# Batch 1 of a 2-D Fourier transform is loaded through a copy in DRAM, the first products change places, and every unit gets a new kind and new due times

## The chip, the cores and the metric

The kernel runs on one core of a Trainium2 chip. Its time is the device time of one execution in microseconds (us); the median of three runs before the change is 599.53 us (598.72 to 600.61). TensorE multiplies matrices, VectorE, ScalarE (ACT) and GpSimd (POOL) work on tiles in the on-chip memory, and SyncE (SP) issues most transfers.

## What is computed

The input x has 8 batches of 3008 rows with 256 numbers. Each batch goes through a 2-D Fourier transform, of which the real part is kept, and then every row goes through a gated feed-forward network (FFN) with 1536 hidden numbers:

```python
X = np.fft.fft(x, axis=1)
X = np.fft.fft(X, axis=2)
x = X.real.reshape(24064, 256)
g = x @ w_gate
out = (g / (1 + np.exp(-g)) * (x @ w_val)) @ w_out
```

## The kernel before

**Transform.** A real transform along 3008 rows has mirror symmetry, so rows are needed in rising and in falling order. For each batch the tile XA takes 128 row pairs of each of four quarters (R = 752 rows): its slots 0 to 3 hold the rising rows, 4 to 7 the falling ones. The partitions run in falling order of the rows, in blocks of LA = 8, so that the rising rows (up_block) are loaded block by block, 8 partitions a transfer (16 transfers of 64 KB), while the falling rows (down_set) take one transfer of 256 KB for each quarter. XC holds the 60 row pairs that remain, in blocks of 4 partitions (15 transfers of 32 KB), even batches in the partitions from 0 and odd ones in those from 64. Batch 1 is an exception: its rows of XC lie in both halves of the partitions, one of each pair of rows in either, which took a copy XC<-XC within the chip at the end (L169). C1_ORDER and A1_ORDER spell the order in which its 25 and 20 transfers are issued.

POOL folds these rows (fold_steps, L171: cross into SDf, even and odd into EOf, ab into Af, ce and bb into the coefficient tiles CEa, BBa and Fc). Fc goes to the stacks St by transfers. TensorE multiplies the coefficients by tables of sines and cosines (Tab), and VectorE adds and subtracts the results into the tiles Pt and Qt (L1411, the puts), the even and odd parts along the 256 numbers. The second transform, along the 256 numbers, is multiplied into the weights: Wp = CD x W and Wq = SDt x W, and Wm = -2 Wq outside of partition 0 (L1442 to L1457 for the later weights; first_w, L499, for the first).

**FFN.** The 12032 columns of Pt and Qt are cut into 24 tiles (480, 512 or, at the end, 320 wide; 8 more columns join the last). A unit is a tile and one of 12 blocks of 128 hidden numbers; there are 288, in order. Each column gives two output rows, a row k of the transform and its mirror. For one unit TensorE adds Wp x Pt and Wq x Qt into g (gate) and v (value), and then Wm x Qt, which turns the sum into the mirror's. ACT applies silu to g (sp, and sv for the mirror), VectorE multiplies sp by v into hp (L1186), and makes the mirror's value from es (L1109, L1175). POOL multiplies the two halves of sv into hm (L1183) for two units at once. TensorE then multiplies hp and hm by Wo into o (L1236), ACT copies o to ev (L1243) and SP stores it (L1249).

KINDS (L928) has one character for each unit, which says how its work is shared out. A "w" is a unit without these shortcuts (6 products on TensorE). For a hex digit, bit 0 (seeded): ACT writes a first row's term into v ahead of the product (L1045) and copies es, in place of a VectorE operation. Bit 1 (gate split): TensorE leaves out one of the three gate products, and VectorE does two operations instead (L1088, L1152). 4 and above: ACT copies v, and POOL makes hp (L1192); 8: POOL makes the mirror's value as well (L1195).

**Order.** The first stage, up to tile 0, is written out by hand (L517 to L649). All later work is given to a planner (Sched, L767): each operation has an engine, an assumed duration and a due time, which is the planned TensorE time so far plus SHIFT for its sort plus BIAS for its sort and tile. The planner walks through the operations and emits, for each engine, one fixed order; on the chip, each engine follows its order and waits for semaphores. There are 3 buffers of g and v, 2 of o in PSUM, 2 of sv and es, 3 of sp, sg and ev. SP has at most 8 transfers under way in this plan. Transfers for weights (load_w, L386; Wo, L1641) are issued on POOL's queue.

In the first stage psC holds two o buffers until VectorE has read them. half_folded(1, 0, False) is the last table product that needs POOL's EOb, row0 adds the row of the heads CEa and CEc, even_copy copies half of the sums to od, and first_puts makes Pt and Qt of tiles 0 and 1. copies are the copies of the first weights out of PSUM.

Of the kernel before, what the change touches and what calls it, by code (L numbers as in the profile page):

```python
# [19 lines left out]
def kernel(  # L20
# [113 lines left out]
    C1_EARLY = 6  # L134
    C1_ORDER = "uuduuduuduuduumuueuueuece"
    A1_ORDER = "uuuuduuuuduuuuduuuud"

    def load_a(b, q):
        X3 = XA.rearrange("p a q d -> p a (q d)")
        res = ([lambda h=h: q.dma_start(out=X3[LA * h:LA * (h + 1), 0:4, :],  # L140
                                         in_=up_block(b, JA - LA * h, LA)) for h in range(NA)] +
                [lambda a=a: q.dma_start(out=X3[:, 4 + a, :], in_=down_set(b, a, JA, LA, NA)) for a in range(4)])
        return in_order(A1_ORDER, u=res[:NA], d=res[NA:]) if b == 1 else res

    def in_order(order, **todo):
        todo = {k: list(v) for k, v in todo.items()}
        return [todo[k].pop(0) for k in order]

    def load_c(b, q):

        X3 = XC.rearrange("p a q d -> p a (q d)")
        p0 = 64 * (b % 2)
        pm = p0 + NCR
        r = slice(p0, p0 + NCR)
        ups = [lambda h=h: q.dma_start(out=X3[p0 + LC * h:p0 + LC * (h + 1), 0:4, :],
                                       in_=up_block(b, JC - LC * h, LC)) for h in range(NC_)]
        mid = [lambda: q.dma_start(out=XC[pm:pm + 1, 0:4, 1],
                                   in_=rows_at(b, 0, [[R * D, 1], [R * D, 4], [1, D]]))]
        if b != 1:
            return ups + [lambda a=a: q.dma_start(out=X3[r, 4 + a, :], in_=down_set(b, a, JC, LC, NC_))  # L160
                          for a in range(4)] + mid

        def down(a, k):
            q.dma_start(out=XC[0:NCR, 4 + a, 0] if k else XC[r, 4 + a, 0],
                        in_=rows_at(b, R * (a + 1) - 2 * JC + k, [[2 * LC * D, NC_], [-2 * D, LC], [1, D]]))

        downs = [[lambda a=a, k=k: down(a, k) for a in range(4)] for k in range(2)]
        return in_order(C1_ORDER, u=ups, d=downs[0], e=downs[1], m=mid,
                        c=[lambda: q.dma_start(out=XC[0:NCR, 0:4, 1], in_=XC[r, 0:4, 0])])  # L169
# [311 lines left out]
    def half_folded(eo, a0, first):  # L481
        for q in range(2):
            for a in range(a0, a0 + 2):
                dst, rhs = set_cols(acc[eo][q], Tab[:, 0, q, eo], a)
                nc.tensor.matmul(dst, EOb[:, eo, a, q, :], rhs, start=first and a == a0, stop=False, skip_group_check=True)
# [58 lines left out]
    for hi in range(2):  # L544
        q.dma_start(out=X3c[64 * hi + NCR:64 * hi + 64, :].rearrange("p (c d) -> p c d", d=D),
                    in_=zeros[64 * hi + NCR:64 * hi + 64].unsqueeze(1).to_broadcast([64 - NCR, 16, D]))
    loads_c1 = load_c(1, q)
    for load in loads_c1[:C1_EARLY]:
        load()
# [22 lines left out]
    half_folded(1, 0, False)  # L572
    load_w(1, (1,))
    heads(Ec0[:, 0], Ec0[:, 1], CEc)
# [167 lines left out]
    )  # L742
    BIAS = {(t, k): v for t, row in enumerate(BIAS_ROWS) for k, v in zip(SHIFT, row)}
# [11 lines left out]
    W_AT = (0.0, 2.0, 3.2, 4.6)  # L755
# [164 lines left out]
    def pool_us(n):  # L920
# [14 lines left out]
        "001601031052",  # L935
        "300171700001",
        "331213005030",
        "010271031001",
        "34130b310300",
        "01b300700101",  # L940
        "21312101b300",
        "001371310011",
        "32120011b212",
        "10130b135030",
        "000135003170",
        "033170001011",
        "213b21011200",
        "103b10319610",
        "4030b13300b0",
        "616404563200",  # L950
        "143034169230",
        "706150233313",
# [343 lines left out]

    def run_loads(n):
        for what, k, fn in loads[:n]:
            up = k < (NA if what[0] == "A" else NC_)
            r, w, us, ring = [], [((what[0],), k)], 0.4 if up else 0.62, 0.57 if up or what[0] == "C" else 1.14  # L1300
            if what == ("A", 1):
                r = [(("C",), C1_ORDER.rindex("u"))]
                us, ring = (0.42, 0.75) if A1_ORDER[k] == "u" else (0.75, 1.1)
            if what == ("C", 1):
                us, ring = (0.48, 0.75) if C1_ORDER[k] == "u" else (0.95, 1.0)
                if C1_ORDER[k] == "c":
                    r = [(("C",), j) for j, o in enumerate(C1_ORDER) if o == "u"]
            S.add("SP", us, fn, r=r, w=w, after=[(("A",), "pre" if A1_ORDER[k] == "d" else "preW")] if what == ("A", 1) else [],
                  lat=2.5, ring=ring)
        del loads[:n]  # L1310
# [4 lines left out]
    def fold_step(what, i, unit):  # L1315
        kind, b = what
        q, j = (1, i) if what == ("C", 1) else divmod(i, 6)
        if i == 0:
            run_loads(max((k + 1 for k, (w_, _, _) in enumerate(loads) if w_ == what), default=0))
# [14 lines left out]
        r = {0: [((kind,), k) for k in range(40)], 1: [(tmp, "F")], 2: [(tmp, "F")], 3: [(tmp, "E"), (tmp, "O")],  # L1334
# [12 lines left out]
    def load_next(what):  # L1347
        kind, b = what
        if kind == "A":
            if b + 1 < B:  # L1350
                loads.extend((("A", b + 1), k, fn) for k, fn in enumerate(load_a(b + 1, nc.sync)))
        else:
            b = b // 2 * 2 + 2
            if b < B:
                loads.extend((("C", b), k, fn) for k, fn in enumerate(load_c(b, nc.sync) + load_c(b + 1, nc.sync)))
# [248 lines left out]
    for k in range(C1_EARLY):  # L1604
        S.add("DMA", 0.01, lambda: None, w=[(("C",), k)], lat=2.0)
# [3 lines left out]
    S.add("DMA", 0.01, lambda: None, w=[(("pq", 0), "Q")], lat=0.1)  # L1609
# [7 lines left out]
    for i, u in enumerate(units):  # L1617
# [49 lines left out]
    S.run({'DVE': 1.6, 'ACT': 1.0, 'POOL': 1.4, 'PE': 0.0, 'SP': 2.0})  # L1667
# [30 lines left out]
```

## Time and profile before

| | |
|---|---|
| median of 3 runs | 599.53 us |
| the profiled execution | 600.4 us |
| its span, first to last instruction | 598.6 us |
| DMA packets, bytes | 51082, 57.65 MB |
| HBM read, written | 29.43 MB, 24.65 MB |

The profile is of one execution. For each engine it gives the busy time; TensorE's matmuls overlap, so that its starts say more than its ends. A row of the timeline has the start and the length, the engine (PE is TensorE, PEld its weight loads, DVE VectorE, SPq SyncE's queue), the line, the tiles out<-in, the shapes and the count; in brackets stands the idle time of the engine before it and what ended it. A row by stretch has, after the stretch and its length, the busy time of PE, PEld, DVE, ACT and POOL with their counts, then the granted TensorE clock (1.00 is full), the busy share of the DMA engines and GB/s. A row of waits has the total, how many there were and the longest.

### The profile page before, as it was taken

To read this page: it belongs to the slowest core of one execution; us is meant where nothing else is said; L and a number is where in the kernel's file an instruction comes from. 1 tells how busy PE (TensorE), PEld (TensorE's weight loads), DVE (VectorE), ACT (ScalarE), POOL (GpSimd) and SP (SyncE) were. 2 spreads that over 40 slices of the span, in tenths; PEclk is the share of its full clock that TensorE was granted. 3 is DMA by queue.
4 is the path that set the end of the run, shared out by engine and by line. 5 is a ranking of instruction groups with operands and counts; after the bars stand their busy time and mean duration, and the time that the engine had idled before them with its cause. 6 is when DMAs were issued, how large, how long until landed. Compare 5 with 4: busy or idle time off the path is not lost.

```text
span 598.6 us, 12468 instructions
## 1 busy us (share of the span) xinstructions
PE 587.0 (98%) x3953; PEld 389.2 (65%) x4012; DVE 570.3 (95%) x1064; ACT 557.4 (93%) x1080; POOL 527.8 (88%) x486
## 2 busy tenths in 40 slices
PE   7999999999999999999999999999999999999997
PEld 5456666666666666666666666666666666666686
DVE  8989999999999999999999999999999999999993
ACT  8778989989998999999999999999999999999995
POOL 8977999999899999998999998897986868687772
PEclk9999999999999999999999999999999999999999
DMA  9956347454715523454127122046221202111212
GB/s 247 150 110 115 109 121 141 132 140 117 178 46 107 136 70 113 123 129 138 57 55 166 46 62 82 19 115 161 63 64 37 65 19 80 48 46 53 60 54 81
DMA packets 51082, 57.65 MB, mean 96 GB/s; under 512 B 7283, under 2 KB 38439, under 8 KB 51017
## 3 DMA queue, kind: packets, MB, share of 16 engines
q1 hardware_dynamic: 47433, 53.91, 35.2%
q0 software_dynamic: 3216, 2.36, 2.8%
q8 instruction: 31, 0.51, 0.4%
q10 hardware_dynamic: 368, 0.59, 0.3%
q14 instruction: 34, 0.28, 0.2%
HBM read 29.43 MB, written 24.65 MB: 90 GB/s over the span
## 4 chain that ended last, share of the span: by engine, by line
PE 71%; ACT 8%; DMA 6%; DVE 4%; POOL 3%; issue 3%; SPq 1%; ACTq 0%; POOLq 0%; DVEq 0%
PE o L1236 30%; PE g L972 19%; PE v L972 16%; DMA XA<-in_x_dram 5%; ACT sv L1159 2%; PE o L1394 2%; PE g L1394 2%; ACT v L1045 2%; ACT es L1107 1%; POOL hm L1183 1%; DVE sv L1175 1%; ACT sp L1084 1%; DVE hp L1186 1%; ACT sp L1156 1%; ACT ev L1243 1%
## 5 line engine op out<-in xcount | busy, mean ns | idle before, releaser
L1183 POOL TENSOR_TENSOR hm<-sv 128x1024 bf16<-128x1024 f32 (+2 forms) x137 | 254.7, 1862 | 44.1 <-ACT sv L1159 17.7
L1175 DVE SCALAR_TENSOR_TENSOR sv<-es,v 128x512 f32<-128x512 f32 (+2 forms) x262 | 173.6, 668 | 5.4 <-PE v L972 2.8
L1236 PE MATMUL o<-Wo,hm 128*128 128x256 bf16 (+1 forms) x1128 | 163.6, 273 | 0.3
L1236 PE MATMUL o<-Wo,hp 128*128 128x256 bf16 (+1 forms) x1104 | 159.7, 273 | 0.2
L1186 DVE TENSOR_TENSOR hp<-sp,v 128x512 bf16<-128x512 f32 (+2 forms) x233 | 154.2, 668 | 2.8 <-PE v L972 2.0
L1236 PEld LDWEIGHTS <-hm 128*128 128x128 bf16 (+2 forms) x1140 | 111.8, 98 | 57.9 <-issue 2.5
L1236 PEld LDWEIGHTS <-hp 128*128 128x128 bf16 (+2 forms) x1140 | 111.9, 98 | 55.8 <-issue 0.9
L1159 ACT ACTIVATE sv<-g 128x512 f32<-128x512 f32 (+2 forms) x179 | 116.7, 671 | 4.6 <-PE g L972 2.3
L1084 ACT ACTIVATE sp<-g 128x512 f32<-128x512 f32 (+2 forms) x179 | 110.5, 621 | 4.1 <-PE g L972 2.7
L972 PE MATMUL v<-Pt,Wp 128*128 128x512 bf16 (+2 forms) x288 | 105.4, 375 | 1.8 <-DVE hp L1186 0.5
L972 PE MATMUL g<-Pt,Wp 128*128 128x512 bf16 (+2 forms) x280 | 104.4, 374 | 0.9 <-ACT sv L1159 0.7
L1045 ACT ACTIVATE v<-bc,w 128x512 f32<-128x512 bf16 (+2 forms) x146 | 104.6, 717 | 0.4
L1109 DVE SCALAR_TENSOR_TENSOR es<-bc,w,v 128x512 f32<-128x512 bf16 (+2 forms) x128 | 92.6, 731 | 2.4 <-ACT bc L1595 0.8
L1107 ACT ACTIVATE es<-v 128x512 f32<-128x512 f32 (+2 forms) x146 | 90.0, 618 | 3.8 <-PE g L972 1.0
L972 PE MATMUL g<-Qt,Wq 128*128 128x512 bf16 (+2 forms) x247 | 90.5, 374 | 0.4
L972 PEld LDWEIGHTS <-Wp 128*128 128x128 bf16 x576 | 56.3, 98 | 27.8 <-DVE Wp L505 0.7
L972 PE MATMUL g<-Qt,Wm 128*128 128x512 bf16 (+2 forms) x186 | 69.8, 375 | 0.2
L1088 DVE SCALAR_TENSOR_TENSOR sg<-bc,w,g 128x512 f32<-128x512 bf16 (+2 forms) x95 | 68.4, 723 | 1.4 <-PE g L972 0.7
L1159 ACT ACTIVATE sv<-sg 128x512 f32<-128x512 f32 (+2 forms) x95 | 65.1, 692 | 0.2 <-DVE sg L1152 0.2
L1152 DVE SCALAR_TENSOR_TENSOR sg<-sg,g 128x512 f32<-128x512 f32 (+2 forms) x95 | 62.9, 662 | 1.5 <-PE g L972 0.8
L1156 ACT ACTIVATE sp<-g 128x512 f32<-128x512 f32 (+2 forms) x95 | 57.7, 608 | 5.5 <-DVE sg L1152 5.3
L972 PE MATMUL v<-Qt,Wm 128*128 128x512 bf16 (+2 forms) x159 | 59.4, 374 | 0.8 <-ACT es L1107 0.4
(218 smaller groups left out, 759.1 us busy)
## 6 DMA issues: line engine op xcount, KB each, us to landing
out_dram<-ev SPq DMA_DIRECT2D x96, 128.0 KB
XA<-in_x_dram SPq DMA_DIRECT2D x30, 256.0 KB
XA<-in_x_dram SPq DMA_DIRECT2D x112, 64.0 KB
XC<-in_x_dram SPq DMA_DIRECT2D x28, 120.0 KB
XC<-in_x_dram SPq DMA_DIRECT2D x105, 32.0 KB
bc<-br SPq DMA_DIRECT2D x19, 128.0 KB
St<-Fc SPq DMA_DIRECT2D x12, 128.5 KB
out_dram<-ev SPq DMA_DIRECT2D x12, 120.0 KB
```

Source lines behind the costliest of these rows:

```text
L972: nc.tensor.matmul(ps[:, :n], Wt[:, gv, fs], src[:, :n], start=start, stop=stop, skip_group_check=True)
L1045: nc.scalar.activation(T_[kv][:, :w], bc[t][:, :w], AF.Copy, scale=w0[:, 1, f:f + 1])
L1084: nc.scalar.activation(sp_to()[:, :w], T_[kg][:, :w], AF.Silu)
L1088: nc.vector.scalar_tensor_tensor(T_[keg][:, :w], bc[t][:, :w], w0[:, 0, f:f + 1], T_[kg][:, :w], op0=Alu.mult, op1=Alu.add)
L1107: nc.scalar.activation(T_[kes][:, :w], T_[kv][:, :w], AF.Copy, scale=2.0 if on_pool(u) > 1 else 1.0)
L1109: nc.vector.scalar_tensor_tensor(T_[kes][:, :w], bc[t][:, :w], w0[:, 1, f:f + 1], T_[kv][:, :w], op0=Alu.mult, op1=Alu.add)
L1156: nc.scalar.activation(sp_to()[:, :wp], T_[kg][:, :wp], AF.Silu)
L1159: nc.scalar.activation(sv()[:, f % 2, w - 1::-1, 1], T_[kgm if by_dve else kg][:, :w], AF.Silu)
L1175: nc.vector.scalar_tensor_tensor(sv()[:, f % 2, w - 1::-1, 0], T_[kes][:, :w], 2.0, T_[kv][:, :w], op0=Alu.mult, op1=Alu.subtract)
L1183: nc.gpsimd.tensor_tensor(hts_(t)[1][:, f - 1:f + 1, :w], sv()[:, :, :w, 1], sv()[:, :, :w, 0], op=Alu.mult)
L1186: nc.vector.tensor_tensor(hts_(t)[0][:, f, :wp], T_[ksp][:, :wp], T_[kv][:, :wp], op=Alu.mult)
L1236: nc.tensor.matmul(st["ps"][:n, j, :], hts[t][minus][:, f, c:c + n], Wo[:, f, :], start=(f == 0), stop=(f == nF - 1))
```

## The change

- **Loads of batch 1.** The rising rows of XA (four copies of 256 KB, one for each quarter) and of XC (four of 120 KB) are copied within DRAM into a scratch tile in which the blocks lie in falling order (turn). XA's rising half then comes in two transfers of 128 partitions (up_a1), XC's in two of 60 (up_c1), straight into the partitions where they belong, so the copy XC<-XC goes. The falling rows stay as they were. Together SP issues 25 transfers in place of 45. The planner gets new durations for all loads.
- **Their place.** Ahead of tile 0 SP issues one of the two clearing transfers, the middle row, four falling loads of XC and the other clearing transfer, where it was both clearing transfers and six loads. The four other falling loads, the eight copies, the two loads of turned XC and XA's six follow in the plan.
- **First stage.** half_cast(0, 2) goes ahead of the two copies of FA. The first value weight's product goes ahead of half_folded(1, 0), which is split by q with row0 in between; its copy (copies[2], VectorE) goes ahead of the Qt sums; turn_signs goes later. On POOL, heads goes ahead of load_w(1, (1,)).
- **Units.** KINDS and BIAS_ROWS are replaced as a whole (the old BIAS_ROWS stays in the file and is overwritten), as are W_AT and the planner's starting times.

```diff
+    def turn(kind, q):
+        L, N, j0 = (LA, NA, JA) if kind == "A" else (LC, NC_, JC)
+        t = scratch[kind] = dram.tile([4, N, 2 * L, D], F32, name=f"turned{kind}")
+        def one(a):
+            q.dma_start(out=t[a].rearrange("h r d -> r h d"),
+                        in_=rows_at(1, R * a + 2 * j0 - 1, [[D, 2 * L], [-2 * L * D, N], [1, D]]))
+        return [lambda a=a: one(a) for a in range(4)]
...
+    def up_a1(a, q):
+        q.dma_start(out=XA.rearrange("p a q d -> p a (q d)")[:, a:a + 2, :],
+                    in_=scratch["A"][a:a + 2].rearrange("a h (i q) d -> (h i) a (q d)", q=2))
+    def down_c1(a, k, q):
+        q.dma_start(out=XC[slice(0, NCR) if k else slice(64, 64 + NCR), 4 + a, 0],
+                    in_=rows_at(1, R * (a + 1) - 2 * JC + k, [[2 * LC * D, NC_], [-2 * D, LC], [1, D]]))
+    def up_c1(k, q):
+        q.dma_start(out=XC[slice(64, 64 + NCR) if k else slice(0, NCR), 0:4, 1],
+                    in_=scratch["C"][:].rearrange("a h (i q) d -> q (h i) a d", q=2)[k])
...
     half_cast(0, 0)
+    half_cast(0, 2)
     for a in range(2, 4):
         nc.scalar.copy(FA[:, a, :, P + 1:D], psA[a][:, :, P + 1:D])
-    half_cast(0, 2)
...
+    clear_c(1)
+    mid_c(1, q)
+    for a in range(4):
+        down_c1(a, 0, q)
+    clear_c(0)
...
+    copies = [first_w(0, 0, 1, psG.tile([P, T], F32, name="g"))]
     folded_c(0, 0)
-    copies = [first_w(0, k, 1, p_.tile([P, T], F32, name=n_)) for k, (p_, n_) in enumerate(((psG, "g"), (psV, "v")))]
+    copies.append(first_w(0, 1, 1, psV.tile([P, T], F32, name="v")))
...
-    half_folded(1, 0, False)
+    copies.append(first_w(1, 0, 0, psO.tile([P, T], F32, name="o")))
+    heads(Ec0[:, 0], Ec0[:, 1], CEc)
     load_w(1, (1,))
-    heads(Ec0[:, 0], Ec0[:, 1], CEc)
...
-    for i in range(2):
-        row0(0, i, acc[1][i])
     copies[0]()
     copies[1]()
+    copies[2]()
+    half_folded(1, 0, False, (0,))
+    row0(0, 0, acc[1][0])
+    od1 = even_copy(1)
+    half_folded(1, 0, False, (1,))
+    row0(0, 1, acc[1][1])
+    copies.append(first_w(1, 1, 1, psO.tile([P, T], F32, name="o")))
+    first_puts(1, od1, (0,))
+    copies[3]()
     turn_signs()
-    od1 = even_copy(1)
-    copies += [first_w(1, k, k, psO.tile([P, T], F32, name="o")) for k in range(2)]
-    first_puts(1, od1, (0,))
-    for c in copies[2:4]:
-        c()
     first_puts(1, od1, (1,))
...
-    W_AT = (0.0, 2.0, 3.2, 4.6)
+    W_AT = (0.0, 2.4, 3.4, 4.6)
...
-        "06ww20001013",
-        "031303160011",
-        "000010312133",
-        "010210112012",
-        "10110b103133",
+        "02ww60003010",
+        "030001330100",
+        "310130310112",
+        "111010000010",
+        "53130b103113",
...
         if i == 1:
-            loads.extend((("C", 1), k, fn) for k, fn in enumerate(loads_c1) if k >= C1_EARLY)
+            c1 = load_ops("C", 1)
+            loads.extend(c1[:4] + turn_ops("C") + turn_ops("A") + c1[4:])
         if i == A1_LOAD:
-            loads[0:0] = ((("A", 1), k, fn) for k, fn in enumerate(load_a(1, nc.sync)))
+            loads[0:0] = load_ops("A", 1)
...
-    S.run({'DVE': 1.6, 'ACT': 1.0, 'POOL': 1.4, 'PE': 0.0, 'SP': 2.0})
+    S.run({'DVE': 1.4, 'ACT': 0.8, 'POOL': 1.6, 'PE': 0.0, 'SP': 2.0})
```

More of the change, by code (lines that the diff above doesn't have):

```diff
@@ L152, in load_c @@
         p0 = 64 * (b % 2)
[L153 to L169, printed above, removed]
+        return ([lambda h=h: q.dma_start(out=X3[p0 + LC * h:p0 + LC * (h + 1), 0:4, :], in_=up_block(b, JC - LC * h, LC))
+                 for h in range(NC_)] +
+                [lambda a=a: q.dma_start(out=X3[p0:p0 + NCR, 4 + a, :], in_=down_set(b, a, JC, LC, NC_)) for a in range(4)] +
+                [lambda: mid_c(b, q)])
     def fold_steps(eng, X, CE, BB, q, r):
@@ L479, in set_cols, with half_folded @@
         return ps[:, 0:NCE], tab[:, 0:NCE]
-    def half_folded(eo, a0, first):
-        for q in range(2):
+    def half_folded(eo, a0, first, qs=(0, 1)):
+        for q in qs:
             for a in range(a0, a0 + 2):
@@ L1318, in fold_step @@
         if i == 0:
-            run_loads(max((k + 1 for k, (w_, _, _) in enumerate(loads) if w_ == what), default=0))
+            run_loads(max((k + 1 for k, (w_, _, _) in enumerate(loads) if w_ == what or kind == w_[0] == "C"), default=0))
         def fn():
@@ L1333, in fold_step @@
         tmp = ("fold",)
-        r = {0: [((kind,), k) for k in range(40)], 1: [(tmp, "F")], 2: [(tmp, "F")], 3: [(tmp, "E"), (tmp, "O")],
+        r = {0: [((kind,), k) for k in [(i, j) for i in range(2) for j in range(20)] + list(range(20))], 1: [(tmp, "F")], 2: [(tmp, "F")], 3: [(tmp, "E"), (tmp, "O")],
              4: [(tmp, "A")], 5: [(tmp, "E"), (tmp, "O")]}[j]
@@ L1350, in load_next @@
             if b + 1 < B:
-                loads.extend((("A", b + 1), k, fn) for k, fn in enumerate(load_a(b + 1, nc.sync)))
+                loads.extend(load_ops("A", b + 1))
         else:
@@ L1354, in load_next @@
             if b < B:
-                loads.extend((("C", b), k, fn) for k, fn in enumerate(load_c(b, nc.sync) + load_c(b + 1, nc.sync)))
+                loads.extend(load_ops("C", b) + load_ops("C", b + 1))
     def spread_op(b):
@@ L1603 @@
     S.hold("st", 0)
-    for k in range(C1_EARLY):
-        S.add("DMA", 0.01, lambda: None, w=[(("C",), k)], lat=2.0)
+    S.add("DMA", 0.01, lambda: None, w=[(("C",), 19)], lat=4.0)
     for fc in (1, 2):
```

96 lines of the change are left out of this document (51 added, 45 removed), and 24 rows, old and new, of the table BIAS_ROWS.

## The prediction

> **What bounds the kernel now.** I read the page's totals first, then the busy times by stretch, then who TensorE waited for, and last the timeline around each wait.
>
> ```profile
> span 598.6 us, 12468 instructions
> PE 587.0 (98%) x3953; PEld 389.2 (65%) x4012; DVE 570.3 (95%) x1064; ACT 557.4 (93%) x1080; POOL 527.8 (88%) x486
> ```
>
> ```profile
> 0.00:18.86 18.86, 15.77 (x104) 9.90 (x106) 16.42 (x68) 14.73 (x25) 17.29 (x40) 1.00 0.89 220
> 18.86:40.00 21.14, 20.83 (x123) 10.07 (x123) 18.86 (x38) 16.95 (x35) 18.56 (x32) 1.00 0.77 135
> 40.00:60.00 20.00, 19.84 (x129) 12.90 (x131) 19.21 (x33) 16.34 (x31) 14.81 (x16) 1.00 0.67 116
> 60.00:120.00 60.00, 58.11 (x394) 38.56 (x396) 56.92 (x105) 54.13 (x106) 59.37 (x57) 1.00 0.50 126
> 120.00:580.00 460.00, 457.20 (x3081) 304.85 (x3129) 449.50 (x803) 443.92 (x858) 411.95 (x341) 1.00 0.33 85
> ```
>
> In each row the second figure is TensorE's busy time, POOL's the sixth. From 18.86 us, where the FFN starts, TensorE hardly stops: 0.6% idle from 120 to 580, but 1.89 of 60 us from 60 to 120, where POOL is full (59.37 of 60). So the time is the first stage (18.86), all products at full pace, and few waits. A change can pay by fewer products, an earlier start, or by removing those waits. The largest of TensorE's own there:
>
> ```profile
> PE g L972 <- ACT sv L1159: 0.7, 1, 0.7
> PE v L972 <- DVE hp L1186: 0.5, 1, 0.5
> PE v L972 <- ACT es L1107: 0.4, 1, 0.4
> ```
>
> A matmul's modelled end overlaps its follower, so idle time understates a wait; I take start-to-start instead:
>
> ```profile
> 19.29 0.36 PE L972 MATMUL g<-Qt,Wq 128*128 128x480 bf16 x1
> 19.89 0.38 PE L972 MATMUL v<-Pt,Wp 128*128 128x480 bf16 x1 [0.24 <-DVE Wp L505]
> 20.11 0.37 PE L972 MATMUL v<-Qt,Wq 128*128 128x480 bf16 x1
> 20.31 0.37 PE L972 MATMUL g<-Qt,Wq 128*128 128x480 bf16 x1
> ...
> 25.05 0.39 PE L1442 MATMUL o<-XA,CD 128*128 128x512 bf16 x1
> 25.50 0.37 PE L972 MATMUL v<-Pt,Wp 128*128 128x480 bf16 x1
> ...
> 63.66 0.38 PE L1591 MATMUL g<-Qt,sel 128*128 128x512 bf16 x1
> 64.74 0.38 PE L972 MATMUL g<-Pt,Wp 128*128 128x512 bf16 x1 [0.70 <-ACT sv L1159]
> 64.96 0.38 PE L972 MATMUL g<-Qt,Wq 128*128 128x512 bf16 x1
> ...
> 79.72 0.59 PE L972 MATMUL v<-Pt,Wp 128*128 128x512 bf16 x2
> 80.86 0.38 PE L972 MATMUL v<-Pt,Wp 128*128 128x512 bf16 x1 [0.55 <-DVE hp L1186]
> ...
> 106.33 0.57 PE L972 MATMUL g<-Qt,Wq 128*128 128x480 bf16 x2
> 107.25 0.36 PE L972 MATMUL v<-Qt,Wm 128*128 128x480 bf16 x1 [0.36 <-ACT es L1107]
> ```
>
> Undisturbed starts lie 0.20 us apart at 480 columns and 0.22 at 512. So the waits are 0.60-0.20 = 0.40 at 19.89, 0.45-0.22 = 0.23 at 25.50, 1.08-0.22 = 0.86 at 64.74, 1.14-0.44 = 0.70 at 80.86 and 0.92-0.41 = 0.51 at 107.25: 2.70 us in all. The two large ones have one root:
>
> ```profile
> 42.33 2.36 POOL L178 TENSOR_TENSOR SDf<-XC 128x1020 f32<-128x1020 f32 x1 [2.06 <-DMA XA<-in_x_dram]
> 44.92 0.82 POOL L1546 COPY Tab<-Tab 64x752 bf16<-64x752 bf16 x1
> ...
> 53.57 0.20 POOL L202 TENSOR_TENSOR Fc<-EOf 128x2 bf16<-128x2 f32 x1
> 59.65 2.36 POOL L178 TENSOR_TENSOR SDf<-XA 128x1020 f32<-128x1020 f32 x1 [2.03 <-DMA out_dram<-ev]
> 62.11 1.90 POOL L1183 TENSOR_TENSOR hm<-sv 128x1024 bf16<-128x1024 f32 x1
> 64.05 0.64 ACT L1159 ACTIVATE sv<-g 128x512 f32<-128x512 f32 x1 [0.88 <-PE g L1591]
> 78.93 1.29 DVE L1175 SCALAR_TENSOR_TENSOR sv<-es,v 128x512 f32<-128x512 f32 x2 [0.71 <-POOL hm L1183]
> ```
>
> POOL stood 2.06 and 2.03 us in front of batch 1's folds, whose inputs are the loads that the change rebuilds (the semaphore named in the second is another transfer's; only XA is new to that instruction). hm then ends at 64.01, sv comes free, ACT starts at 64.05, and TensorE gets its g buffer. At 78.93 DVE again waits for an hm.
>
> **The change part by part.** *Products.* Counting the unit codes, 95 units were gate-split and 89 are; each split saves one gate product and costs VectorE two operations. Nine 512-wide splits go; two of 512 and one of 320 come. Net 7 x 0.217 - 0.14 = +1.38 us of TensorE, with nothing to hide it. The same count gives VectorE 11 operations fewer (at 0.66 about 7 us of 570), ACT 6 fewer, POOL 4 more (5 us of 528, most in tiles 10 and 21, where POOL has idle time).
>
> *First stage.*
>
> ```profile
> 16.82 0.48 PE L485 MATMUL g<-Tab,EOb 128*128 128x377 bf16 x2
> 17.23 0.33 PE L613 MATMUL v<-Tab,CEa 128*1 128x189 bf16 x2
> 17.73 0.33 PE L613 MATMUL g<-Tab,CEc 128*1 128x189 bf16 x2
> 17.98 0.60 PE L502 MATMUL o<-W,CD 128*128 128x512 bf16 x2
> ```
>
> Two products at 0.16 from 16.82 end at 17.14, two at 0.08 from 17.73 at 17.89: about 0.2 us of gaps, which the new order fills (the value weight's first product goes ahead, and CEc is made before POOL's weight issue). All products are the same, so the FFN starts near 18.66: -0.2 (bounds 0 and -0.3). Wp's value half is now copied before the Qt sums, with VectorE free from about 17.7, so the 0.40 wait goes: -0.4 (bounds 0, -0.4).
>
> *Weights.* POOL issues the last three weight loads behind two small operations more (both heads, like L461 here):
>
> ```profile
> 15.81 0.73 POOL L391 DMA_DIRECT2D XA<-in_moe_w_val_dram  x1
> 16.57 0.21 POOL L461 TENSOR_TENSOR CEc<-Ec 128x2 bf16<-128x2 f32 x1
> ...
> DMA to landing us min/median/max: 7.4/8.2/9.8
> ```
>
> The first of them was out at 15.81 and lands after 7.4; at 16.15 it lands at 23.55. In the new order its product follows 16 products of 0.20 and four of 0.22, at 18.66+4.1 = 22.8. TensorE's order is fixed, so everything behind would stand 0.75 us, or 0 if the load gets faster because SP issues less: I take +0.4. The later 0.23 (the next weights) is then covered: -0.23.
>
> *Loads of batch 1.* SP issued 25 transfers for XC and 20 for XA; now 9 for XC at first hand, 4+4 copies within DRAM (480 KB and 1 MB), 2 loads of turned C, 4 falling and 2 turned A loads: 25. No row shows a copy within DRAM. Its bounds are the pace of the wide early transfers, 220 GB/s (first row above), and that of the 64 KB blocks that go:
>
> ```profile
> 48.24 3.60 SPq L140 DMA_DIRECT2D XA<-in_x_dram  x4
> ...
> Wo<-in_moe_w_out_dram POOLq DMA_DIRECT2D x1, 768.0 KB, 12.0
> ```
>
> 256 KB in 3.60 us is 73 GB/s. 1.5 MB of copies then take 7 or 21 us; behind 11 issues from 13.92 (0.9 each) they start near 23.5. I take about 11 us, since they share the engines with Wo until 35 but are wide; then 2.6 MB at some 200 GB/s: XC by 38, XA near 50 (bounds 43 and 66). Setup keeps POOL until 42.33-2.06 = 40.27, and 41.1 with the table copy (0.82 at 44.92) that now comes ahead of C's fold; the fold with one hm inside took 53.77-42.33-0.82 = 10.6, so POOL asks for XA at 51.7. Both waits, 4.1 us, are then gone. XA's fold comes some 8 us earlier than 59.65. Behind SP's wait for the copies stand the XA loads, C2's loads and the first stores, whose three ev buffers ACT fills; the first store was not needed before 55. So -0.86, -0.70 (bounds 0 and these), and half of 0.51: ACT was late there, and by the codes it loses some 3 us of work in tile 2 and gains as much in tile 3: -0.25 (bounds 0, -0.51).
>
> *Due times of all units.* They can't be costed row by row. Outside these waits TensorE's idle time is 0.6%, 2.8 us from 120 to 580; VectorE's 7 us less lets me take -0.2 (bounds -1.2 and +1.5, half of that idle time either way).
>
> The sum: 1.38-0.2-0.4+0.4-0.23-0.86-0.70-0.25-0.2 = -1.06. The profiled execution took 600.4 (span 598.6), so 599.3; it lay 0.9 above the median of the runs, so **598.4 us**.
>
> **The rivals.** *The loads come late (slower).* If XA lands after 51.7, POOL stands in order, hm behind it, then sv, g and TensorE as at 64.74. Before it lost 4.1 us there and TensorE 1.56; from about 56 on it is worse than before. At the 116 GB/s of the 40-to-60 row the 4.1 MB from 23.5 need 35 us: 58.5, 7 us lost, 3 more than before, plus the 1.38, less 0.4: about 603.4. For it: that row's pace, and Wo's 12 us. Against: those were narrow blocks. In the Trainium skill, "DMA: Bandwidth & Descriptors", section "Anatomy of one DMA", a transfer carries about 2 us of fixed cost, most of it the receipt of the last write, heaviest where the target is HBM; by that estimate the second hop adds about 2 us once (XA at 52), too little for this rival. No row here shows such a receipt by itself.
>
> *The waits stay, from VectorE and ACT.* At 95% and 93% they may hold TensorE wherever POOL did; then only 1.38-0.4 is left: 600.5. Against: the chain of 64.05 starts at hm.
>
> *ACT in tile 5.* Its codes go from 10110b103133 to 53130b103113, about three ACT operations more (2 us), in a stretch where ACT has none to spare:
>
> ```profile
> 140.00:160.00 20.00, 19.84 (x135) 13.13 (x137) 18.67 (x39) 19.94 (x40) 19.67 (x19) 1.00 0.58 127
> ```
>
> If half isn't absorbed, 599.4.
>
> *All goes.* The unit order also closes half of the late idle time and no weight is late: 598.4-1.2-0.4 = 596.8.
>
> **How the numbers follow.** About 0.3% (1.8 us) is what a measurement of this kernel can tell from no change, so faster means below 597.7. Forecast 0.40 (its own range 597.2 to 599.6, 0.16 of it below 597.7), all goes 0.26, waits stay 0.13, tile 5 0.07, late loads 0.14. Faster 0.16+0.26 = 0.42; slower 0.14 and a little of waits-stay, 0.16; same 0.42. The range goes from 596.2 to 601.8, which leaves out most of late loads and the best tail.
>
> **What would show it.** Right: SDf<-XC on POOL near 41 and SDf<-XA by 52 without a DMA wait; no TensorE wait over 0.5 us between 60 and 90; FFN start at 18.7; six products more. Wrong: POOL standing at SDf<-XA beyond 56; TensorE waiting for a weight product near 23 by more than 0.8, or for Wo near 41; ACT full and TensorE waiting for es or sv from 135 to 165.

## The result and the profile after

The changed kernel takes 602.65 us (median of 6 runs, 602.27 to 603.84); the kernel before took 600.07 in the same comparison (6 runs, 598.28 to 601.46). The ratio is 1.0049 with an interval of 1.0026 to 1.0072: slower by 0.5%, where 598.4 was predicted. The profiled execution took 603.73.

First the totals of the changed kernel (span, then busy time, share and number of instructions of each engine), and two of the stretches shown before:

```profile
span 602.0 us, 12426 instructions
PE 591.2 (98%) x3958; PEld 390.7 (65%) x4018; DVE 564.8 (94%) x1053; ACT 554.6 (92%) x1074; POOL 532.5 (88%) x490
...
18.86:40.00 21.14, 20.82 (x125) 10.16 (x124) 18.59 (x41) 17.13 (x35) 18.43 (x34) 1.00 0.93 192
120.00:580.00 460.00, 456.55 (x3052) 302.01 (x3102) 443.31 (x787) 438.69 (x844) 413.09 (x341) 1.00 0.33 85
```

VectorE's work fell by 5.5 us (about 7 were counted), and the loads moved up: 192 GB/s from 18.86 to 40, where it was 135. From 120 on TensorE shows 0.8% of idle time, where it was 0.6%; more on that figure below. POOL's folds of batch 1 and TensorE's first FFN products in the timeline:

```profile
45.44 2.35 POOL L186 TENSOR_TENSOR SDf<-XC 128x1020 f32<-128x1020 f32 x1 [3.85 <-DMA XC<-turnedC]
55.96 2.35 POOL L186 TENSOR_TENSOR SDf<-XA 128x1020 f32<-128x1020 f32 x1 [0.22 <-DMA out_dram<-ev]
...
19.42 0.57 PE L1012 MATMUL g<-Pt,Wp 128*128 128x480 bf16 x2
20.26 0.59 PE L1492 MATMUL o<-XA,CD 128*128 128x512 bf16 x2 [0.27 <-ACT Wq L513]
```

XA's fold no longer waits (0.22 in place of 2.03) and comes 3.7 us earlier. XC's fold is 3.1 us later than before, not earlier. The FFN starts at 19.42, not at 18.66, and 0.84 - 0.41 = 0.43 us behind its first two products TensorE waits for an o buffer, where 0.40 at 19.89 was to go. SP's queue shows why XC is late (in the last row, what it waited for):

```profile
13.80 0.77 SPq L553 DMA_DIRECT2D XC<-Z  x1
19.70 0.63 SPq L156 DMA_DIRECT2D XC<-in_x_dram  x1
...
29.52 2.73 SPq L142 DMA_DIRECT2D turnedC<-in_x_dram  x4
...
SPq L156 <- DMA XC<-Z: 5.0, 1, 5.0
```

The middle row (19.70) is written into partitions that the clearing transfer at 13.80 writes too. SP stood 5.1 us for that, and the copies started 6 us later than the 23.5 that I took.

### The profile page after: what moved, and what is told of

The parts are those of the page before. It is cut to its first block, busy times and chain, and to the rows that moved or that the text cites. A ratio compares the mean times of both kernels' runs of the same rounds, so it can differ in the third digit from the quotient of the medians.

```text
span 602.0 us, 12426 instructions
## 1 busy us (share of the span) xinstructions
PE 591.2 (98%) x3958; PEld 390.7 (65%) x4018; DVE 564.8 (94%) x1053; ACT 554.6 (92%) x1074; POOL 532.5 (88%) x490
## 4 chain that ended last, share of the span: by engine, by line
PE 84%; DVE 4%; ACT 3%; issue 3%; DMA 3%; POOL 1%; SPq 1%; ACTq 0%; POOLq 0%; DVEq 0%
PE o L1276 35%; PE g L1012 22%; PE v L1012 19%; PE g L1444 2%; PE o L1444 2%; DVE sv L1215 2%; DMA XC<-in_x_dram 1%; DVE es L1149 1%; ACT sv L1199 1%; ACT es L1147 1%; DMA out_dram<-ev 1%; DVE hp L1226 1%; POOL hm L1223 1%; PE v L1276 1%; PE o L1492 1%
## 5 line engine op out<-in xcount | busy, mean ns | idle before, releaser
L1199 ACT ACTIVATE sv<-g 128x512 f32<-128x512 f32 (+2 forms) x185 | 123.1, 677 | 5.4 <-PE g L1012 3.2
L1124 ACT ACTIVATE sp<-g 128x512 f32<-128x512 f32 (+2 forms) x185 | 115.2, 630 | 3.0 <-PE g L1012 1.7
L1085 ACT ACTIVATE v<-bc,w 128x512 f32<-128x512 bf16 (+2 forms) x141 | 102.1, 725 | 2.8 <-DVE sv L1215 1.4
L1149 DVE SCALAR_TENSOR_TENSOR es<-bc,w,v 128x512 f32<-128x512 bf16 (+2 forms) x133 | 97.3, 736 | 2.4 <-PE v L1012 1.0
L1012 PE MATMUL g<-Qt,Wm 128*128 128x512 bf16 (+2 forms) x195 | 73.0, 376 | 0.5 <-ACT sp L1124 0.3
L1199 ACT ACTIVATE sv<-sg 128x512 f32<-128x512 f32 (+2 forms) x89 | 62.0, 697 | 3.6 <-DVE sg L1192 2.5
L1128 DVE SCALAR_TENSOR_TENSOR sg<-bc,w,g 128x512 f32<-128x512 bf16 (+2 forms) x89 | 64.1, 722 | 0.7 <-PE g L1012 0.5
L1192 DVE SCALAR_TENSOR_TENSOR sg<-sg,g 128x512 f32<-128x512 f32 (+2 forms) x89 | 58.7, 660 | 2.8 <-PE g L1012 2.1
L1012 PEld LDWEIGHTS <-Wq 128*128 128x128 bf16 x435 | 42.4, 98 | 28.8 <-issue 3.0
L1283 ACT COPY ev<-o 128x512 f32<-128x512 f32 x89 | 55.3, 622 | 3.5 <-PE o L1276 3.3
```

The source lines that it names most:

```text
L1012: nc.tensor.matmul(ps[:, :n], Wt[:, gv, fs], src[:, :n], start=start, stop=stop, skip_group_check=True)
L1085: nc.scalar.activation(T_[kv][:, :w], bc[t][:, :w], AF.Copy, scale=w0[:, 1, f:f + 1])
L1124: nc.scalar.activation(sp_to()[:, :w], T_[kg][:, :w], AF.Silu)
L1128: nc.vector.scalar_tensor_tensor(T_[keg][:, :w], bc[t][:, :w], w0[:, 0, f:f + 1], T_[kg][:, :w], op0=Alu.mult, op1=Alu.add)
L1149: nc.vector.scalar_tensor_tensor(T_[kes][:, :w], bc[t][:, :w], w0[:, 1, f:f + 1], T_[kv][:, :w], op0=Alu.mult, op1=Alu.add)
L1192: nc.vector.scalar_tensor_tensor(T_[kgm][:, :w], T_[keg][:, :w], 2.0, T_[kg][:, :w], op0=Alu.mult, op1=Alu.subtract)
```

## The experiments

The theories that the expectations name: T, the loss lies in the new kinds and due times. R, the new loads of batch 1 cost it (the route through DRAM, or their lateness). F, the new order of the first stage costs it. All times are medians, ratios are to the kernel before, run on the same chip beside them.

| kernel | loads | units | first stage | us | ratio, 95% interval |
|---|---|---|---|---|---|
| before, again | old | old | old | 599.79 | 1.0002 (0.9989 to 1.0014) |
| new loads, old units | new | old | old | 598.53 | 0.9982 (0.9972 to 0.9991) |
| old first stage | new | new | old | 602.69 | 1.0049 (1.0031 to 1.0068) |
| changed kernel | new | new | new | 602.65 | 1.0049 (1.0026 to 1.0072) |
| middle row last | new, mended | new | new | 602.40 | 1.0050 (1.0038 to 1.0062) |

**Units against loads, by exchanging them whole.** Two kernels: the changed one with KINDS and BIAS_ROWS of before, and the kernel before with those of the change.

```diff
 # the changed kernel
-        "02ww60003010",
-        "030001330100",
+        "06ww20001013",
+        "031303160011",
...
-        (0.7, -5.05, -12.55, -2.25, 11.45, -27.35, -34.35, 25.8, 26.55, 21.8, 28.65, 3.65, -10.1, -19.05, 5.25, 0.55, 2.45),
...
```

> The changed kernel with the kinds and due times of before (95 gate splits), its new loads and first stage kept. The plan of all engines is made anew from them. Theory T (the loss lies in the new kinds and due times: 1.38 us of products and some 2 us of new waits behind 120 us): 2 to 3.5 us below the changed kernel, so 599 to 600.7 against 602.65, within 0.2% of before. Rival R (the loads of batch 1 cost it): only the products go, 601.3 or more, and the waits in the first 100 us stay.

> The kernel before with the kinds and due times of the change, its old loads and first stage kept. Theory T: 602 to 604 against 600.1 for the kernel before, with the new products and the waits between 150 and 250 us as in the changed kernel. Rival R: 600 to 601.4, the products alone.

They took 626.83 and 613.13 us, ratios 1.0461 (1.0444 to 1.0478) and 1.0227 (1.0214 to 1.0240). Neither theory had expected that. In the stretch from 120 to 580, where neither loads of batch 1 nor the first stage act any more (first row: old units in the changed kernel; second: new units in the kernel before), TensorE is idle for 11.7 and 5.4 us:

```profile
120.00:580.00 460.00, 448.34 (x2953) 287.14 (x2952) 427.64 (x759) 421.78 (x804) 392.29 (x326) 1.00 0.32 83
120.00:580.00 460.00, 454.56 (x3035) 295.19 (x3033) 434.71 (x769) 429.34 (x822) 406.56 (x336) 1.00 0.32 83
```

A set of due times serves the one plan that it was made with: by its code the planner walks through another order as soon as a load's assumed duration differs (this was not run by itself), and 13 to 27 us against the kernel before hang on the exchange. So exchanging them tells nothing on T or R; from here on the finished order of the engines was kept, and instructions were replaced or moved within it.

**The middle row last.** SP's order alone: `clear_c(1), clear_c(0), 4 x down_c1, mid_c`.

```diff
     clear_c(1)
-    mid_c(1, q)
+    clear_c(0)
     for a in range(4):
         down_c1(a, 0, q)
-    clear_c(0)
+    mid_c(1, q)
```

> The changed kernel with SP's early order changed alone: both clearing transfers, then the four falling loads, and the middle row last, so that its wait for the clearing transfer has the falling loads in front of it. All other engines keep their order. SP's standstill from 14.57 to 19.70 should shrink to 1 us or so, the copies start 4 us earlier, and the fold SDf<-XC start near 42 in place of 45.44. Theory T: the time moves by -0.7 to +0.3, as TensorE lost little at these folds. Rival R (the late loads cost it): at least 2 us faster than the changed kernel, 600.6 or less.

SP's queue in this run:

```profile
15.27 5.89 SPq L159 DMA_DIRECT2D XC<-in_x_dram  x4
21.26 0.65 SPq L156 DMA_DIRECT2D XC<-in_x_dram  x1
```

The standstill did not vanish: 2.4 us of it lie within the four falling loads now (5.89 us for what takes 3.5 elsewhere), but the copies start 4.0 us earlier (25.51) and SDf<-XC at 42.3. The time is 602.40 (602.25 to 602.84): in the median, no difference that can be told from none. Two of the six executions of the changed kernel took 603.73 and 603.84, though, and the profiled one of them (603.73) has a wait that the trace of this run lacks:

```profile
70.02 0.38 PE L1012 MATMUL v<-Qt,Wm 128*128 128x512 bf16 x1 [0.57 <-ACT es L1147]
```

It comes 0.95 us after its predecessor, a wait of 0.73. ACT had stood 1.14 us for an hm, and POOL reached this hm at 66.92 in place of 64.83. So the late XC cost nothing in most executions, and by this one trace near 1 us in some. This run has all of its 4018 matmul records, so it serves as the base of what follows.

**The old route under the new plan.** No copies within DRAM; the rising rows in 16 and 15 blocks as before, at the place of the new loads.

> The changed kernel with the old route of the rising rows alone: no copies within DRAM, XA's rising rows as 16 blocks and XC's as 15 blocks with the copy within the chip, at the place of the new loads and in the same plan of all other engines. Theory T (the new route takes up to 1 us of waits out of 40 to 100 us, as hoped): 0 to 1.5 us slower than the changed kernel. Rival R (the route through DRAM costs it): 1.5 us or more faster than the changed kernel.

611.20 us (606.67 to 613.27), 8.5 above the changed kernel, far more than T's 0 to 1.5; its waits (first XC's fold, then TensorE):

```profile
POOL SDf L191 <- DMA XC<-in_x_dram: 7.4, 1, 7.4
PE v L1017 <- DVE es L1154: 7.7, 1, 7.7
```

The plan needs the new route. R is refuted in this form; how much the route is worth by itself, this run can't say, since the old blocks stand at places made for the new ones.

**The new route under the old plan.** The kernel before; its rising loads replaced in their places, all orders of TensorE, VectorE, ACT and POOL kept. And the kernel before once more, for a second profile.

```diff
-        return in_order(C1_ORDER, u=ups, ..., c=[lambda: q.dma_start(out=XC[0:NCR, 0:4, 1], in_=XC[r, 0:4, 0])])
+        none = [lambda: None]
+        ups = none * 4 + turn("C", q) + turn("A", q) + none + [lambda: up_c1(1, q), lambda: up_c1(0, q)]
+        return in_order(C1_ORDER, u=ups, d=downs[0], e=downs[1], m=mid, c=none)
...
+        ups = [lambda: up_a1(0, q), lambda: up_a1(2, q)] + [lambda: None] * (NA - 2)
```

> The kernel before with the new loads of batch 1 alone (eight copies within DRAM, two loads of turned XC, two of turned XA, the falling loads as they were) in the places of the old ones, and with the finished order of TensorE, VectorE, ACT and POOL unchanged, kinds and due times included. Theory T (the new route pays what the sum took, 1.56 to 1.8 us, and the new units cost more than that): SDf<-XC near 41, SDf<-XA near 53, the waits of 0.86 and 0.70 gone, 597.7 to 598.5. Rival R (the route through DRAM brings nothing or costs): 599.5 or more. This would be faster than both kernels.

> The kernel before, unchanged, for a second profile and for what its own times scatter. The first profile lay 0.9 above its median. If the waits at 64.74 and 80.86 (1.56 us there) belong to every execution, they are here within 0.2; if they hang on how late batch 1's loads land in one execution, they are smaller in a profile nearer the median, and the gain that the sum took was too large by that.

The new loads with the old units take 598.53 us (11 runs, 598.32 to 598.91), 1.1 below the kernel before (599.66, 23 runs) and 4.1 below the changed kernel: faster than both. The second profile of the kernel before first, in its totals, its last stretch, POOL's fold of XA and TensorE at the place where it had waited 0.86 us; then both folds with the new loads; at the end a third profile with the old loads and orders, that of the products run below:

```profile
span 597.7 us, 12527 instructions
PE 591.2 (99%) x4012; PEld 390.4 (65%) x4012; DVE 570.3 (95%) x1064; ACT 558.1 (93%) x1080; POOL 528.2 (88%) x486
...
120.00:580.00 460.00, 459.98 (x3129) 304.81 (x3128) 449.43 (x803) 443.73 (x857) 412.04 (x340) 1.00 0.32 85
...
58.95 2.36 POOL L178 TENSOR_TENSOR SDf<-XA 128x1020 f32<-128x1020 f32 x1 [0.43 <-DMA out_dram<-ev]
...
64.77 0.38 PE L1591 MATMUL g<-Qt,sel 128*128 128x512 bf16 x1
64.99 0.38 PE L972 MATMUL g<-Pt,Wp 128*128 128x512 bf16 x1
```

```profile
40.15 2.34 POOL L203 TENSOR_TENSOR SDf<-XC 128x1020 f32<-128x1020 f32 x1
55.61 1.89 POOL L1208 TENSOR_TENSOR hm<-sv 128x1024 bf16<-128x1024 f32 x1 [2.04 <-DVE sv L1200]
57.46 2.36 POOL L203 TENSOR_TENSOR SDf<-XA 128x1020 f32<-128x1020 f32 x1
```

```profile
59.85 2.36 POOL L178 TENSOR_TENSOR SDf<-XA 128x1020 f32<-128x1020 f32 x1 [1.94 <-DMA XC<-in_x_dram]
...
63.95 0.38 PE L1592 MATMUL g<-Qt,sel 128*128 128x512 bf16 x1
64.94 0.38 PE L973 MATMUL g<-Pt,Wp 128*128 128x512 bf16 x1 [0.61 <-ACT sv L1160]
```

Three things are to be seen. In the second execution of the same kernel before, XA's fold waits 0.43 us and TensorE's products at 64.77 and 64.99 lie 0.22 apart: the wait of 0.86, and the one at 80.86, are not there. In the third they are back, 0.99 - 0.22 = 0.77 and, at 81.08, 0.73. So they come in some executions and not in others: the FFN started at 18.86 and 19.18 where they came and at 19.82 where they didn't, with XA's fold at 59.65, 59.85 and 58.95. Then, the same kernel's TensorE is busy for 591.2 us, not 587.0, with 59 matmuls more, and for 459.98 of the 460 us from 120 on: the first profile lacks records, and the 0.6% idle that I read there was missing rows. Last, with the new loads POOL waits for neither fold; its wait goes to an hm instead (2.04 for VectorE's sv), and costs nothing.

**The old first stage.** The changed kernel with the first stage in the old order, plan and loads kept. And three mends in the new one: the middle row last, o buffers exchanged, half_folded in one piece.

```diff
+    psO.at = 1 - psO.at
     copies.append(first_w(1, 0, 0, psO.tile([P, T], F32, name="o")))
...
-    half_folded(1, 0, False, (0,))
+    half_folded(1, 0, False)
     row0(0, 0, acc[1][0])
     od1 = even_copy(1)
-    half_folded(1, 0, False, (1,))
```

> The changed kernel with the first stage in the old order (both first weights behind folded_c, half_folded(1, 0) unsplit, row0 ahead of the copies, turn_signs early, heads behind the weight issue); loads, kinds, due times and the plan kept. Rival F (the new first-stage order costs it): FFN start 0.2 us earlier and the 0.43 us wait at 20.26 gone, 602.0 or less. Theory T (the first stage neither gains nor loses by its order, since the 0.4 us only changes place): 602.4 with 0.5 either way.

> The changed kernel with three mends ahead of 25 us: the middle row last on SP (as in the run before), the two o buffers exchanged ahead of first_w(1, 0) so that the product behind 19.6 takes the one that VectorE frees early, and half_folded(1, 0) in one piece again. The plan of what follows is kept. Expected from the trace: the wait of 0.43 us at 20.26 gone, FFN start 0.15 us earlier, so 0.5 us below the kernel with the middle row last alone, about 601.9; if the wait is owed to ACT's copy whichever buffer is taken, no difference.

602.69 and 602.45 us: no difference. F is refuted (with the old order the wait of 0.43 is there too, at 20.07), and the mends bring nothing. The timeline of TensorE in the mended one:

```profile
18.90 0.57 PE L1012 MATMUL g<-Pt,Wp 128*128 128x480 bf16 x2
19.30 0.59 PE L1492 MATMUL o<-XA,CD 128*128 128x512 bf16 x2
...
20.95 0.59 PE L1492 MATMUL o<-XA,SDt 128*128 128x512 bf16 x2
21.80 0.36 PE L1012 MATMUL g<-Qt,Wm 128*128 128x480 bf16 x1 [0.25 <-ACT sg L1047]
...
22.20 0.36 PE L1012 MATMUL g<-Qt,Wq 128*128 128x480 bf16 x1
22.62 0.36 PE L1012 MATMUL v<-Qt,Wm 128*128 128x480 bf16 x1
```

The product at 19.30 follows at once: the wait for the o buffer is gone and the FFN starts 0.24 us earlier than with the middle row last alone (19.14). But at 21.80 TensorE waits 0.85 - 0.43 = 0.42 us for ACT and at 22.62 another 0.22. Both runs issue their last twelve products (g<-Wo,hm) at 595.5. In this one case the stall of 0.4 us that was taken out turned up at a later product that needs ACT.

**Products.** The kernel before with 38 gate products issued twice.

```diff
-        nc.tensor.matmul(ps[:, :n], Wt[:, gv, fs], src[:, :n], start=start, stop=stop, ...)
+        for _ in range(2 if start and gv == 0 and n == 512 and u[1] in (5, 8) and 3 <= u[0] <= 22 else 1):
+            nc.tensor.matmul(ps[:, :n], Wt[:, gv, fs], src[:, :n], start=start, stop=stop, ...)
```

> The kernel before with the first gate product of 38 units (blocks 5 and 8 of the tiles 3 to 22, 512 columns) issued twice; the second starts the sum anew, so only time is added, at 0.217 us each, and every other order is kept. If a product costs its full length, as the sum took for the six that the change adds: 8.2 us, 607.9. If VectorE and ACT set the pace from 120 on and the products only fill TensorE's idle time: 3 us or less, below 603.

607.39 us against 599.98, 1.0121 (1.0099 to 1.0143): 7.4 us for 38 products, 0.195 each, 90% of their length (72 to 105% by the interval). TensorE sets the pace, and a product costs nearly its full length.

**What makes the waits from 150 to 200 us.** Comparing the middle row last with the new loads and old units, start by start (what a start comes later than the one before plus its columns at 2400 per us and 0.0035, where that is over 0.03), TensorE's waits behind the FFN's start are 5.25 and 3.05 us; from 150 to 200 they are 1.81 and 0.11. TensorE's, VectorE's, ACT's and POOL's busy time there, old units (second profile of before), then new, and then the new ones around the largest waits:

```profile
150.00:210.00 60.00, 60.00 (x412) 39.68 (x410) 59.05 (x117) 56.71 (x110) 56.87 (x50) 1.00 0.45 117
...
150.00:210.00 60.00, 59.50 (x398) 38.39 (x397) 57.46 (x114) 54.05 (x102) 52.78 (x46) 1.00 0.53 114
...
185.13:194.39 9.26, 8.76 (x52) 4.88 (x51) 9.17 (x15) 9.16 (x17) 9.26 (x8) 1.00 0.53 81
```

All four engines do less in the same 60 us, but around the waits VectorE, ACT and POOL are all full. With the new units POOL is busy for 4.65 of 10 us from 160 to 170 and for all of 180 to 190, and VectorE for 9.9 and 10.0 of 10 in the two stretches from 180 to 200. Five runs took these apart, all on the kernel with the middle row last: a POOL fold moved ahead of one hm, two neighbours on ACT exchanged, four VectorE products cut to 64 columns, two POOL fold steps left out, and an ACT copy moved.

```diff
+            x = next(k for k, o in enumerate(order) if o.eng == "POOL" and ("cp", 3) in o.owners)
+            y = max(k for k in range(x) if order[k].eng == "POOL")
+            order.insert(y, order.pop(x))
```

> The kernel with the middle row last, and in the finished plan one POOL instruction moved: the first fold of batch 3 (SDf<-XA, 171.0 us) goes ahead of the hm at 169.1, in front of which POOL stands 2.3 us. All else keeps its order. Theory T2 (the new assumed durations of the later loads make the plan put this fold later than its data, POOL is empty from 160 to 170 and full from 172 to 200, and TensorE pays): SDf starts near 166.9, POOL runs 2 us earlier up to 185, and TensorE's waits between 150 and 200 (1.81 us) fall by 0.5 to 1.3, so 601.1 to 601.9. Rival (VectorE, full from 190 to 200, sets these waits): they stay within 0.2, 602.4.

> The kernel with the middle row last, and two neighbours on ACT exchanged in the finished order: silu of the first gate of tile 7 (sp, 189.6) goes ahead of the sv of tile 6 (189.0). Its gate is ready at 188.6. Theory T3 (the waits of 0.48, 0.27 and 0.24 us from 190 to 193 lie in the order that the new due times give ACT here): the first falls to below 0.2, the three together by 0.4 to 0.8. Rival (VectorE, full from 190 to 200, sets them): the first goes, the others grow by as much, and the sum of the waits from 150 to 200 stays within 0.2 of 1.81.

> The kernel with the middle row last; VectorE's products hp of four units of tile 6 (180 to 186 us) write 64 of 512 columns, the rest being cleared by POOL at 167, where it stands idle (this leaves out 4 x 448 columns of a product). All orders are kept; VectorE has some 1.9 us less to do ahead of 186. Theory T4 (the waits of 1.81 us between 150 and 200 come from VectorE, which the new kinds leave without a gap from 171 to 200): the three waits from 189.5 to 191.4, 0.98 us, shrink below 0.4, the sum by 0.7 or more, about 601.5. Rival T5 (POOL or ACT sets them): the sum stays within 0.3 of 1.81.

> The kernel with the middle row last, without two of batch 3's fold steps on POOL (185.45 and 188.35, 1.09 us each; this leaves out the even and odd sums of its second half), so that POOL's hm in between come 1.1 and 2.2 us earlier. Theory T4 (VectorE sets the waits behind 189): they stay within 0.3 of 1.81 us. Rival T5 (POOL, full from 171 to 200, sets them): the three from 189.5 to 191.4 shrink below 0.4, the sum by 0.7 or more.

> The kernel with the middle row last; on ACT, in the finished order, the sp of tile 7's first unit goes ahead of tile 6's last sv, and the copy ev<-o of 187.8 goes behind the two sp (to some 190). ACT runs back to back from 186.5 to 194, and TensorE's waits at 189.5, 190.2 and 191.1 end with its operations. Theory T6 (ACT's local queue, in the order that the new due times give, sets these waits): the three together fall from 0.98 to 0.5 or less and the sum from 150 to 200 by 0.4 or more. Rival (they come from the plan's whole run of dependent steps there, gate, sg, sv, gate buffer, so that an exchange only moves them): the sum stays within 0.2 of 1.81.

| run | us | waits, 150 to 200 |
|---|---|---|
| middle row last | 602.40 | 1.81 |
| POOL's fold earlier | 602.90 | 1.96 |
| ACT's neighbours exchanged | 602.89 | 1.93 |
| 1.9 us less on VectorE | 602.59 | 1.82 |
| 2.2 us less on POOL | 602.75 | 1.82 |
| ACT's copy behind | 606.21 | 5.13 |

In the three traces that lack matmul records (the last three rows) the gaps of just one missing product are left out. The 1.96 and 1.93 hold a wait of 0.14 that in the first row begins just ahead of 150. Most of the 5.13 is one stall and the slow clock behind it (see the last section).

With the fold moved, POOL (first two rows, the fold and an hm behind it) only waits at another place; with VectorE relieved (next three rows, VectorE; then TensorE), it does so too:

```profile
167.57 2.35 POOL L186 TENSOR_TENSOR SDf<-XA 128x1020 f32<-128x1020 f32 x1 [0.55 <-DMA out_dram<-ev]
175.49 1.89 POOL L1226 TENSOR_TENSOR hm<-sv 128x1024 bf16<-128x1024 f32 x1 [1.47 <-ACT sv L1202]
```

```profile
184.44 0.22 DVE L1231 TENSOR_TENSOR hp<-sp,v 128x64 bf16<-128x64 f32 x1 [0.40 <-PE v L1012]
185.30 1.28 DVE L1219 SCALAR_TENSOR_TENSOR sv<-es,v 128x512 f32<-128x512 f32 x2 [0.64 <-POOL hm L1227]
186.75 0.75 DVE L1130 SCALAR_TENSOR_TENSOR sg<-bc,w,g 128x512 f32<-128x512 bf16 x1 [0.17 <-PE g L1012]
...
189.30 0.38 PE L1012 MATMUL g<-Pt,Wp 128*128 128x512 bf16 x1
189.99 0.38 PE L1012 MATMUL g<-Qt,Wm 128*128 128x512 bf16 x1 [0.32 <-ACT sp L1126]
```

The time won on VectorE is mostly spent again in front of TensorE's v, POOL's hm and TensorE's g (1.21 us in these rows), before 187; at 189.99 TensorE waits 0.69 - 0.22 = 0.47 us as ever. With ACT's two instructions exchanged, TensorE's rows read:

```profile
189.86 0.38 PE L1015 MATMUL g<-Pt,Wp 128*128 128x512 bf16 x1
190.07 0.38 PE L1015 MATMUL g<-Qt,Wm 128*128 128x512 bf16 x1
190.95 0.38 PE L1015 MATMUL g<-Pt,Wp 128*128 128x512 bf16 x1 [0.50 <-ACT sp L1199]
```

The wait between the first two is gone, and the one behind them has grown from 0.27 to 0.88 - 0.22 = 0.66. Putting ACT's copy ev<-o behind the two sp made TensorE stand 2.3 us for the o buffer that this copy frees. T2, T3 and T6 did not come out; T4 fell when VectorE was relieved, and T5, as far as it names POOL, when POOL was. So these waits are neither VectorE's load nor POOL's, by themselves: in this stretch each engine waits for the order of another. What T5 says of ACT is not tested: ACT, which ends the wait at 190, was only put in another order, its load never lightened. Which kind or due time of tiles 6 and 7 made that order was not tried, since any change of one remakes the whole plan (as the first two runs show); it stays open.

## Why the prediction was wrong

**The starting point.** The sum took 0.86 + 0.70 + 0.25 = 1.81 us of waits out of the profiled execution and then 0.9 more, for that execution's distance from the median. With the new loads and the old units the profiled execution, whose FFN starts as early (18.91 and 18.86), takes 598.53 us, 1.87 below 600.4, and that is also the median: the 1.81 was right for that execution, and the 0.9 counted part of it twice. Against the median of before, in whose executions the waits come or don't, all loads together bring 1.1 us (598.53 against 599.66). The step "So -0.86, -0.70" holds as mechanism: with the new loads POOL waits for no fold and nothing is left of those waits. The scatter of the runs fits this: 3.1 us before (598.21 to 601.28), 0.6 with the new loads.

**Due times of all units**, "-0.2 (bounds -1.2 and +1.5)": the step that failed. The loads alone brought -1.1, the first stage 0, and the new units with the plan made from them +4.2 (602.69 against 598.53). By the traces, from the new loads with old units to the middle row last (last twelve products at 591.63 and 595.48, 3.85 us), that is 0.23 of a later FFN start, 1.36 of products (3264 columns more at 2400 per us) and 2.20 of waits, 1.70 of them from 150 to 200; these make 3.79, 0.06 too little. So where the sum had -0.2 for the due times the runs showed +2.2, new waits of TensorE on engines whose order the new plan set. My bounds were half of TensorE's idle time from 120 to 580, and that idle time was missing records: in the complete trace it is 0.02 us. Counted from start to start, 1.8 us of short waits are left there, so there was little to gain, and no row bounded the loss: due times put into another plan cost 13 to 27 us.

**Products**, +1.38: right. 38 products cost 90% of their length, so little hid them.

**First stage**, -0.2 and -0.4: wrong in both, and worth nothing. The gaps that I read as a wait for CEc stand where weights of 128 columns and of one column change, and the new order has two such changes more. The timeline of the changed kernel:

```profile
17.29 0.48 PE L493 MATMUL v<-Tab,EOb 128*128 128x377 bf16 x2
17.71 0.33 PE L625 MATMUL v<-Tab,CEa 128*1 128x189 bf16 x2
17.87 0.33 PE L625 MATMUL v<-Tab,CEc 128*1 128x189 bf16 x2
18.13 0.49 PE L493 MATMUL g<-Tab,EOb 128*128 128x377 bf16 x2
```

Two products of 0.157 take 0.42 to the next start, two of 0.08 take 0.26 where a wide one follows, but 0.16 where it is of their own kind: 0.1 us for each change. The start itself scatters more than the effect (18.86 and 19.82 in two profiles of before). The wait of 0.40 came back as 0.43 at an o buffer that ACT frees, and as 0.42 and 0.22 elsewhere when that was mended.

**Weights**, +0.4 and -0.23: a product o<-XA,CD near 24 waits 0.31 and 0.17 us in two of the traces with the new plan and not at all in the others, the changed kernel's among them; the +0.4 was too much. The wait of 0.23 at 25.50 was never there: ahead of it the first profile has one o<-XA,CD (25.05), the second one two, and the next product follows without a wait.

```profile
25.85 0.59 PE L1442 MATMUL o<-XA,CD 128*128 128x512 bf16 x2
```

**Loads**, "XC by 38, XA near 50": XC was late in the changed kernel because SP stood for its middle row, which I had overlooked when I let the copies start near 23.5; issued in the old places they start at 19.52 and XC waits for nothing at 40.15. The copies within DRAM, taken as 11 us, were read back 7.2 us (XC, 36.67) and 10.1 us (XA, 39.65) after the first was issued (29.52). The rival that the loads come late fell: XA's fold came at 55.96 without a wait to speak of, and 3 us of lateness at XC cost nothing in the median, though near 1 us in one trace. The rival that the waits stay gave 600.5 for a reason that didn't hold: the waits at 64.74 and 80.86 went. The rival of tile 5 fell too: from 140 to 160 TensorE's waits are 0.43 us in the run with the middle row last, 0.17 with the old units.

## What to carry to other kernels

Take a second and a third profile before pricing a wait that ends with a transfer, since it can come in some executions only, and never subtract both the wait and the profiled execution's distance from the median. Look at the number of matmuls before reading a share of idle time: a count below that of the instructions issued makes idle time, and waits of one product's length, out of missing rows. Due times made for one plan are worth their price only in that plan; where part of a change can be put into the finished order of the old one, as the new loads here, that is the version to run first (598.53 us).

## What the hardware showed

A gap of TensorE of 2.3 us can already cost clock. When ACT's copy was moved, TensorE stood from 189.34 to 191.60; the products behind it started 0.43 us apart in place of 0.22, until some 195.3. The timeline of TensorE and the row of this stretch (granted clock third from the end):

```profile
191.60 1.83 PE L1284 MATMUL o<-Wo,hp 128*128 128x256 bf16 x8 [2.26 <-ACT ev L1291]
193.22 0.63 PE L1020 MATMUL g<-Pt,Wp 128*128 128x512 bf16 x1
193.65 0.63 PE L1020 MATMUL g<-Qt,Wm 128*128 128x512 bf16 x1
...
190.00:200.00 10.00, 8.34 (x43) 4.88 (x44) 6.84 (x12) 7.11 (x15) 8.08 (x7) 0.83 0.82 142
```

So a stall of 2.3 us, the slow clock with it, added 3.8 us to the median (606.21 against 602.40), and waits of 0.9 us, as at 64.74 before, left the pace alone. Of this kernel's five executions two show a mean clock of 0.997 (606.28 and 606.21) and three 1.000 (606.68, 605.65, 605.10); whether the stall was as long in these three isn't known. In the changed kernel with the old units, one gap of 1.30 us, ended at 323.60, left the clock at 1.00 (323 to 328), while two of 1.58 and 0.74, ended at 357.27 and 358.38, were followed by 0.50 from 359.5 to 361.4. In the Trainium skill, "TensorE: Matmul & The Clock Gate", section "HAM oscillation — how this bites in real kernels", the rule is that no gap above some 3.4 us may occur; here 2.3 were enough, so the trace doesn't agree with that figure.
